# Attention and routed experts on one core: queries kept in a permuted token order, copied out of PSUM in runs of eight

## The chip, the cores and the metric

The kernel runs on one core of one Trainium2 chip. The core has a matrix engine (PE, with its weight loads shown apart as PEld), a vector engine (DVE), an activation engine (ACT), a general engine (POOL, here the issuer of most loads) and a queue engine (SP, which issues the stores). Operands lie in SBUF, 128 partitions wide; matmul results land in PSUM and are copied out by DVE or ACT. The metric is the device time of one execution in microseconds; the figure compared is the median of the runs. Lower is better.

## The reference

Two stages in a row. First attention over 8 batches, 8 heads, 576 tokens and head size 64, with a causal window of 128 tokens and a distance bias per head; then its output, laid out as 4608 tokens by 512, goes through 8 experts. Every expert runs on every token, and the results are added with routing weights that come from eight rounds of row and column normalisation.

```python
scores = scale * np.matmul(q, k.transpose(0, 1, 3, 2))
bias = slopes[:, None, None] * (-np.abs(rel).astype(np.float32))[None, :, :]
mask = (rel >= 0) & (rel < window)
scores = np.where(mask, scores + bias[None], -1000000000.0)
...
attn = attn / (np.sum(attn, axis=-1, keepdims=True) + 1e-09)
return np.matmul(attn, v).astype(np.float32)
...
P = np.exp(logits)
for _ in range(8):
    P /= P.sum(1, keepdims=True) + 1e-09
    P /= P.sum(0, keepdims=True) + 1e-09
    P *= N / E
for e in range(E):
    h = np.maximum(x @ w1[e], 0.0)
    ye = h @ w2[e]
    out += P[:, e:e + 1] * ye
```

The order in which the tokens are held inside is free as long as the rows come out at their places: the experts treat every row alike, and the row sums and column sums of the routing don't depend on the order of the rows.

## The kernel before

**Attention stage.** The work is cut into 40 blocks: 8 batches (b) times 5 key blocks (kb) of 128 keys, the last of 64. Block (b, kb) computes the scores of its keys against the 256 queries from its first key on, so the scores stand with keys on the partitions and queries in the columns (L201). ACT takes the exponential (L209), DVE multiplies by a mask that holds both the window and the bias (L215); the mask `maskT` is a constant of 128 keys by 256 query columns per head, built on the host (L50 to L56). Heads go in two halves of four, and one PSUM tile `psS` serves both halves in turn, so the second half's scores wait for the first half's exponential. One block later the probabilities are multiplied with v (`attend`, L245); the sum of the row comes out as an extra column, DVE takes its reciprocal (L253) and scales (L254) into `xsb`, PE turns `xsb` round (L285) and DVE copies the result into the long-lived `xT` (L294), which holds the tokens in columns for the experts. `gates` (L270) makes the routing logits of 128 tokens as soon as their part of `xT` stands.

**Queries and keys of the next batch.** POOL's queue loads q and k in halves of four heads as tiles `qf` and `kf` (L136), `RT` = 6 tokens per partition, 96 partitions. `turn` (L160, DVE) brings each to a layout in which one token slot of two heads is a block of 128 columns; `tr_unit` (L171) then makes six transposes of 96 x 128 into one PSUM tile `psT`, whose columns run over (slot r, partition i), while the token is 6 i + r. The copies out of PSUM put the tokens into order: ACT copies the keys into `KT` (L180), DVE copies the queries in two halves of 64 partitions into `QZ` (L185, L189), a tile that keeps a zero half for each head of a pair. These copies read `psT` in one run and write every element six elements (12 bytes) from the last one:

```python
out=QZ[0:64, j, 0, :].rearrange("p (i r) -> p r i", r=RT),
in_=psT[0:64],
```

In each batch but the last, blocks kb = 1 to 4 each carry one key unit and one query unit of the next batch, and `turn` follows blocks 0 and 2. Batch 0's own units stand at the start of the program.

**What fills the gaps.** The first expert (e = 0) needs only `xT` and its weights, so its pieces are cut in during the attention stage: a first-layer piece (four matmuls and a Relu on ACT, L92, L99) counts 1, a second-layer piece (eight matmuls of L106 and a DVE copy into the accumulator, L307) counts 2, and each block may spend a credit of `RATE` = 3.45 on them at three places (`fill`). The order of instructions on each engine is the order written in this loop; nothing rearranges it there. The small PSUM tiles (`psT`, `psG`, `psXT`, `psh`, `psy`) share four buffers with the tag `pmm`.

**Expert stage.** After the attention stage come the eight rounds of routing on DVE and POOL, the rest of expert 0, and experts 1 to 7, in groups of 512 tokens: first layer, then per 128 tokens a second layer whose result DVE multiplies by the routing weight and adds to the accumulator (L475). The accumulator of 36 blocks of 128 tokens lies in `acc_lo` (`NHI` = 28 blocks, present from the start) and `acc_hi` (8 blocks, opened after the attention stage). With the last expert each block is stored by one DMA of 256 KB on SP's queue (L484).

Of the kernel before, what the change touches and what calls it, by code (L numbers as in the profile page):

```python
# [14 lines left out]
def kernel(  # L15
# [27 lines left out]
    NPR = H // 2  # L43
    RT = 6
    RATE = 3.45
    RP = S // RT
    scale = float(1.0 / np.sqrt(Dh))

    slopes = 2.0 ** (-8.0 * (np.arange(H, dtype=np.float64) + 1.0) / H)
    _kr = np.arange(P)[:, None, None]  # L50
    _jq = np.arange(2 * P)[None, None, :]
    _rel = _jq - _kr
# [7 lines left out]
    xT = per.tile([P, NDT, Ntok], FP16, name="xT")  # L60
    NHI = 28
    acc_lo = per.tile([P, NHI, HD], FP32, name="acc_lo")
    accs: list = [acc_lo]

    def acc(blk: int):
        return acc_lo[:, blk, :] if blk < NHI else accs[1][:, blk - NHI, :]

    P_sb = per.tile([P, NBLK, E], FP32, name="P_sb")
# [49 lines left out]
    with (  # L118
# [47 lines left out]
        def tr_unit(b: int, nm: str, j: int):  # L166
# [12 lines left out]
            if nm == "k":  # L179
                nc.scalar.copy(  # L180
                    out=KTs[b % 2][:, j, :].rearrange("p (i r) -> p r i", r=RT), in_=psT
                )
            else:
                QZ = QZs[b % 2]
                nc.vector.tensor_copy(  # L185
                    out=QZ[0:64, j, 0, :].rearrange("p (i r) -> p r i", r=RT),
                    in_=psT[0:64],
                )
                nc.vector.tensor_copy(  # L189
                    out=QZ[64:128, j, 1, :].rearrange("p (i r) -> p r i", r=RT),  # L190
                    in_=psT[64:128],
                )
# [106 lines left out]
        def add_group(g: int):  # L299
# [9 lines left out]
            for ft in range(NFT):  # L309
                moe.append((1, lambda ft=ft: l1(ft)))  # L310
            if 4 * g < NHI:
                for ms in range(4):
                    moe.append((2, lambda ms=ms: l2(ms)))
# [96 lines left out]
    with (  # L410
# [28 lines left out]

        for g in range(NG - 2, NG):  # L440
            if g not in hT0:
                hT0[g] = new_hT(0, g, per, "hT", 2)
                for ft in range(NFT):
                    l1_piece(0, g, ft, hT0[g], mps, "psh", 3)
            for ms in range(4):
                psy = l2_mm(0, g, ms, hT0[g], mps, "psy", 4)
                nc.vector.tensor_copy(out=acc(4 * g + ms), in_=psy)
        for e in range(1, E):
# [13 lines left out]
            def emit_l2(g, e=e, hTs=hTs):  # L462
                hT = hTs.pop(g)
                for ms in range(4):
# [18 lines left out]
                    if e == E - 1:  # L483
                        nc.sync.dma_start(  # L484
                            out=out[P * blk : P * blk + P, :], in_=acc(blk)
                        )

# [37 lines left out]
```

## Time and profile before

| what | us |
|---|---|
| median of 3 runs (lowest to highest) | 1250.34 (1248.87 to 1253.21) |
| the profiled execution's own time | 1252.59 |
| its span, first to last instruction | 1250.8 |
| PE busy | 1135.5 (91%) |
| DVE busy | 497.6 (40%) |
| ACT busy | 478.6 (38%) |
| POOL busy | 72.5 (6%) |

The profiled execution lies 2.25 us above the median and 1.8 us above its own span. A matmul's end is modelled, so PE's busy time is not work at PE's peak. In names such as `psT_q_0_1027` the last number is a buffer's, the numbers before it say which piece it is: `psS_1_0_966` is the score tile of kb = 1, first half. Lines L1 to L520 are those of the kernel before. In the view of waits and in the timeline the square brackets hold the idle time of the engine just ahead of an instruction and what ended it.

### The profile page before, as it was taken

How to read it: one execution, taken by the hardware profiler on the slowest of the kernel's cores; microseconds unless marked ns; L12 is line 12 of the kernel's file. 1: busy time of each engine (PE TensorE's matmuls, PEld its weight loads, DVE VectorE, ACT ScalarE, POOL GpSimd, SP SyncE). 2: the span in 40 equal slices, each digit the busy share in tenths (PEclk: the TensorE clock that was granted, in tenths of full speed). 3: DMA queues.
4: the chain of work that ended last, by engine and by line, in shares of the span. 5: the costliest groups of instructions: out<-in, count | busy, mean ns of one | idle time of the engine just before them, and what ended most of it. 6: DMA issues, size and time to landing. Idle time of an engine off the chain costs nothing.

```text
span 1250.8 us, 14241 instructions
## 1 busy us (share of the span) xinstructions
PE 1135.5 (91%) x6032; PEld 530.7 (42%) x6032; DVE 497.6 (40%) x754; ACT 478.6 (38%) x725; POOL 72.5 (6%) x101
## 2 busy tenths in 40 slices
PE   2577678767799999999999999999999999999998
PEld 1334334333344444444444444444444444444443
DVE  7867887778658124122212121212121212121212
ACT  3544445545426430433243324332433243323331
POOL 3212021201000000000000000000000000000000
PEclk9997898888899999999999999999999999999999
DMA  9843354335032020200220022002200220001212
GB/s 137 91 39 40 38 57 38 39 39 63 1 56 47 1 34 1 34 1 1 35 34 1 1 34 34 1 1 35 33 1 1 35 33 1 1 1 56 79 68 101
DMA packets 68912, 41.85 MB, mean 33 GB/s; under 512 B 39536, under 2 KB 60016, under 8 KB 68848
## 3 DMA queue, kind: packets, MB, share of 16 engines
q0 software_dynamic: 63376, 30.95, 20.1%
q1 hardware_dynamic: 5472, 10.00, 2.1%
q8 instruction: 47, 0.77, 0.3%
q14 instruction: 17, 0.14, 0.0%
HBM read 62.44 MB, written 9.44 MB: 57 GB/s over the span
## 4 chain that ended last, share of the span: by engine, by line
PE 81%; DVE 15%; ACT 1%; DMA 1%; issue 1%; POOL 0%; POOLq 0%
DVE QZ_76 L189 3%; DVE QZ_76 L185 3%; DVE QZ_75 L189 2%; DVE QZ_75 L185 2%; DVE xT L294 1%; DVE acc_lo L307 1%; DMA w1t_103<-in_moe_w_dram 1%; DMA kf_0_82<-in_k_dram 0%; POOL vsb_77 L148 0%; PE psy_24_3032 L106 0%; PE psy_20_2623 L106 0%; PE psy_28_3420 L106 0%; PE psy_14_1943 L106 0%; PE psy_2_774 L106 0%; PE psy_19_2362 L106 0%
## 5 line engine op out<-in xcount | busy, mean ns | idle before, releaser
L92 PEld LDWEIGHTS <-w1t_103 128*128 128x128 f16 x288 | 29.1, 109 | 57.9 <-issue 29.1
L92 PEld LDWEIGHTS <-w1t_2981 128*128 128x128 f16 x288 | 28.2, 98 | 34.0
L92 PEld LDWEIGHTS <-w1t_6000 128*128 128x128 f16 x288 | 28.2, 98 | 34.0
L92 PEld LDWEIGHTS <-w1t_6805 128*128 128x128 f16 x288 | 28.2, 98 | 34.0
L92 PEld LDWEIGHTS <-w1t_7610 128*128 128x128 f16 x288 | 28.2, 98 | 34.0
L92 PEld LDWEIGHTS <-w1t_3549 128*128 128x128 f16 x288 | 28.2, 98 | 34.0
L92 PEld LDWEIGHTS <-w1t_4390 128*128 128x128 f16 x288 | 28.2, 98 | 34.0
L92 PEld LDWEIGHTS <-w1t_5195 128*128 128x128 f16 x288 | 28.2, 98 | 34.0
L270 PEld LDWEIGHTS <-xT 128*128 128x128 f16 x144 | 7.0, 100 | 59.0 <-DVE xT L294 56.1
L201 PEld LDWEIGHTS <-KT_73 128*128 128x128 f16 (+1 forms) x80 | 7.8, 113 | 27.4 <-issue 21.0
L148 POOL DMA_DIRECT2D vsb_77<-in_v_dram x20 | 16.9, 867 | 0.4 <-issue 0.4
L148 POOL DMA_DIRECT2D vsb_78<-in_v_dram x20 | 16.9, 868 | 0.0
L99 ACT ACTIVATE hT_0_4394<-psh_0_0_4395 128x512 f16<-128x512 f32 x1 | 0.6, 597 | 41.8 <-PE psh_0_0_4395 L92 41.8
L201 PEld LDWEIGHTS <-KT_74 128*128 128x128 f16 (+1 forms) x80 | 7.0, 105 | 10.7 <-issue 7.2
L467 DVE TENSOR_SCALAR acc_lo<-acc_lo,P_sb 128x512 f32<-128x512 f32 x28 | 11.2, 478 | 0.0
L201 PE MATMUL psS_0_0_158<-QZ_75,KT_73 128*128 128x512 f16 x2 | 1.2, 586 | 6.9 <-DVE QZ_75 L189 6.9
L201 PE MATMUL psS_0_1_202<-QZ_75,KT_73 128*128 128x512 f16 x2 | 1.2, 584 | 6.9 <-DVE QZ_75 L189 6.9
L171 PE MATMUL psT_k_0_124<-ident,kp_0_120 96*128 96x96 f16 x6 | 0.7, 277 | 7.3 <-DVE kp_0_120 L160 7.3
L81 POOL DMA_DIRECT2D w1t_7610<-in_moe_w_dram x1 | 0.8, 752 | 110.1 <-PE psh_8_7_7524 L92 110.1
L81 POOL DMA_DIRECT2D w1t_6805<-in_moe_w_dram x1 | 0.8, 754 | 109.6 <-PE psh_8_7_6719 L92 109.6
L81 POOL DMA_DIRECT2D w1t_6000<-in_moe_w_dram x1 | 0.8, 752 | 109.6 <-PE psh_8_7_5914 L92 109.6
L81 POOL DMA_DIRECT2D w1t_5195<-in_moe_w_dram x1 | 0.8, 752 | 109.6 <-PE psh_8_7_5109 L92 109.6
(2900 smaller groups left out, 2638.7 us busy)
## 6 DMA issues: line engine op xcount, KB each, us to landing
out_dram<-acc_lo SPq DMA_DIRECT2D x28, 256.0 KB, 2.0
vsb_77<-in_v_dram POOLq DMA_DIRECT2D x16, 128.0 KB, 4.7
vsb_78<-in_v_dram POOLq DMA_DIRECT2D x16, 128.0 KB, 5.0
out_dram<-acc_hi SPq DMA_DIRECT2D x8, 256.0 KB, 2.0
w1t_103<-in_moe_w_dram POOLq DMA_DIRECT2D x1, 1024.0 KB, 8.5
w2t_113<-in_moe_w_dram POOLq DMA_DIRECT2D x1, 1024.0 KB, 11.3
w1t_2981<-in_moe_w_dram POOLq DMA_DIRECT2D x1, 1024.0 KB, 9.6
w2t_3362<-in_moe_w_dram POOLq DMA_DIRECT2D x1, 1024.0 KB, 9.1
```

Source lines behind the costliest of these rows:

```text
L81: nc.gpsimd.dma_start(out=w1ts[e], in_=w1v)
L92: nc.tensor.matmul(out=psh, lhsT=w1t[:, dt, P * ft : P * ft + P], rhs=xT[:, dt, GT * g : GT * g + GT], start=(dt == 0), stop=(dt == NDT - 1),)
L99: nc.scalar.activation(out=hT[:, ft, :], in_=psh, func=AF.Relu)
L148: nc.gpsimd.dma_start(out=vsb[0:nk, kb, :, 0:Dh], in_=v[b, :, k0 : k0 + nk, :].rearrange("h s d -> s h d"),)
L171: nc.tensor.matmul(out=psT[:, r, :], lhsT=tt[:, r, 2 * Dh * jj : 2 * Dh * jj + 2 * Dh], rhs=ident[0:RP, 0:RP], is_transpose=True, start=(r ...
L185: nc.vector.tensor_copy(out=QZ[0:64, j, 0, :].rearrange("p (i r) -> p r i", r=RT), in_=psT[0:64],)
L189: nc.vector.tensor_copy(out=QZ[64:128, j, 1, :].rearrange("p (i r) -> p r i", r=RT), in_=psT[64:128],)
L201: nc.tensor.matmul(out=ps[0:nk, jj, :, 0:nq], lhsT=KT[:, 2 * half + jj, k0 : k0 + nk], rhs=QZ[:, 2 * half + jj, :, k0 : k0 + nq],)
L270: nc.tensor.matmul(out=psG, lhsT=xT[:, dt, P * blk : P * blk + P], rhs=wg_sb[:, dt, :], start=(dt == 0), stop=(dt == NDT - 1),)
L294: nc.vector.tensor_copy(out=xT[:, :, t0 : t0 + nk], in_=psXT[:, :, 0:nk])
L307: nc.vector.tensor_copy(out=acc(4 * g + ms), in_=psy)
L467: nc.vector.tensor_scalar(out=acc(blk), in0=acc(blk), scalar1=P_sb[:, blk, 0:1], scalar2=None, op0=ALU.mult,)
```

## The change

`RT` goes from 6 to 8, so q and k are loaded with 8 tokens on each of 72 partitions, and a unit is eight transposes of 72 x 128. `KT` keeps the keys in their own order: ACT now walks `psT` as (i, r), reading two bytes every 144 bytes, and writes one run of 576. `QZ` holds the queries permuted inside each block of 64 tokens: position 8 r + i of a block holds its token 8 i + r. DVE then reads `psT` in its own order and writes runs of 8 elements (16 bytes). The mask's columns take the same permutation; everything behind it (probabilities, `xT`, routing, accumulators) carries its rows in that order, and `store` puts each block of 64 rows back with a DMA of its own, so 72 stores of 128 KB stand in place of 36 of 256 KB. The larger q and k tiles take 5 KB more of each partition; `acc_lo` gives up one block (`NHI` 27), and the second-layer piece of block 27 of expert 0 moves behind the attention stage.

```diff
@@ -41,14 +41,19 @@
     GT = 512
     NG = Ntok // GT
     NPR = H // 2
-    RT = 6
+    RT = 8
+    HB = 64
+    NHB = S // HB
+    HI = HB // RT
     RATE = 3.45
     RP = S // RT
     scale = float(1.0 / np.sqrt(Dh))
 
     slopes = 2.0 ** (-8.0 * (np.arange(H, dtype=np.float64) + 1.0) / H)
+    _pos = np.arange(2 * P)
+    _tok = (_pos // HB) * HB + (_pos % HI) * RT + (_pos % HB) // HI
     _kr = np.arange(P)[:, None, None]
-    _jq = np.arange(2 * P)[None, None, :]
+    _jq = _tok[None, None, :]
     _rel = _jq - _kr
     maskT_np = np.where(
         (_rel >= 0) & (_rel < P), np.exp(-slopes[None, :, None] * _rel), 0.0
@@ -58,12 +63,20 @@
 
     per = ctx.enter_context(tc.tile_pool(name="per", bufs=1))
     xT = per.tile([P, NDT, Ntok], FP16, name="xT")
-    NHI = 28
+    NHI = 27
     acc_lo = per.tile([P, NHI, HD], FP32, name="acc_lo")
     accs: list = [acc_lo]
 
     def acc(blk: int):
         return acc_lo[:, blk, :] if blk < NHI else accs[1][:, blk - NHI, :]
+
+    def store(blk: int):
+        for c in range(P // HB):
+            t0 = P * blk + HB * c
+            nc.sync.dma_start(
+                out=out[t0 : t0 + HB, :].rearrange("(i r) d -> r i d", r=RT),
+                in_=acc(blk)[HB * c : HB * c + HB, :],
+            )
 
     P_sb = per.tile([P, NBLK, E], FP32, name="P_sb")
     ident = per.tile([P, P], FP16, name="ident")
@@ -178,17 +191,18 @@
                 )
             if nm == "k":
                 nc.scalar.copy(
-                    out=KTs[b % 2][:, j, :].rearrange("p (i r) -> p r i", r=RT), in_=psT
+                    out=KTs[b % 2][:, j, :].rearrange("p (i r) -> p i r", r=RT),
+                    in_=psT.rearrange("p r i -> p i r"),
                 )
             else:
                 QZ = QZs[b % 2]
                 nc.vector.tensor_copy(
-                    out=QZ[0:64, j, 0, :].rearrange("p (i r) -> p r i", r=RT),
-                    in_=psT[0:64],
+                    out=QZ[0:64, j, 0, :].rearrange("p (c r i) -> p r c i", r=RT, i=HI),
+                    in_=psT[0:64].rearrange("p r (c i) -> p r c i", i=HI),
                 )
                 nc.vector.tensor_copy(
-                    out=QZ[64:128, j, 1, :].rearrange("p (i r) -> p r i", r=RT),
-                    in_=psT[64:128],
+                    out=QZ[64:128, j, 1, :].rearrange("p (c r i) -> p r c i", r=RT, i=HI),
+                    in_=psT[64:128].rearrange("p r (c i) -> p r c i", i=HI),
                 )
 
         def scores(b: int, kb: int, half: int):
@@ -308,8 +322,8 @@
 
             for ft in range(NFT):
                 moe.append((1, lambda ft=ft: l1(ft)))
-            if 4 * g < NHI:
-                for ms in range(4):
+            for ms in range(4):
+                if 4 * g + ms < NHI:
                     moe.append((2, lambda ms=ms: l2(ms)))
 
         credit = 0.0
@@ -437,12 +451,12 @@
                 op1=ALU.mult,
             )
 
-        for g in range(NG - 2, NG):
+        for g in range(NHI // 4, NG):
             if g not in hT0:
                 hT0[g] = new_hT(0, g, per, "hT", 2)
                 for ft in range(NFT):
                     l1_piece(0, g, ft, hT0[g], mps, "psh", 3)
-            for ms in range(4):
+            for ms in range(max(0, NHI - 4 * g), 4):
                 psy = l2_mm(0, g, ms, hT0[g], mps, "psy", 4)
                 nc.vector.tensor_copy(out=acc(4 * g + ms), in_=psy)
         for e in range(1, E):
@@ -481,9 +495,7 @@
                         op1=ALU.add,
                     )
                     if e == E - 1:
-                        nc.sync.dma_start(
-                            out=out[P * blk : P * blk + P, :], in_=acc(blk)
-                        )
+                        store(blk)
 
             lead = LEAD if e == 1 else 1
             for g in range(min(lead, NG)):
```

On DVE, block (2, 1) of the attention stage. Before (the names ahead of `<-` are written, those behind it read):

```order
L160 COPY qp_0_959<-qf_0_801 96x1536
L215 TENSOR_TENSOR pt_1_0_969<-pt_1_0_969,maskT 128x1024
L215 TENSOR_TENSOR pt_1_1_981<-pt_1_1_981,maskT 128x1024
L253 RECIPROCAL rden_0_0_1004<-psN_2_0_999 128x4
L254 TENSOR_TENSOR xsb_0_998<-psN_2_0_999,rden_0_0_1004 128x256
L253 RECIPROCAL rden_0_1_1012<-psN_2_0_1007 128x4
L254 TENSOR_TENSOR xsb_0_998<-psN_2_0_1007,rden_0_1_1012 128x256
L185 COPY QZ_76<-psT_q_0_1027 64x6x96
L189 COPY QZ_76<-psT_q_0_1027 64x6x96
L294 COPY xT<-psXT_0_1036 128x4x128
```

and now:

```order
L173 COPY qp_0_1007<-qf_0_845 72x2048
L229 TENSOR_TENSOR pt_1_0_1017<-pt_1_0_1017,maskT 128x1024
L229 TENSOR_TENSOR pt_1_1_1029<-pt_1_1_1029,maskT 128x1024
L267 RECIPROCAL rden_0_0_1054<-psN_2_0_1049 128x4
L268 TENSOR_TENSOR xsb_0_1048<-psN_2_0_1049,rden_0_0_1054 128x256
L267 RECIPROCAL rden_0_1_1062<-psN_2_0_1057 128x4
L268 TENSOR_TENSOR xsb_0_1048<-psN_2_0_1057,rden_0_1_1062 128x256
L199 COPY QZ_76<-psT_q_0_1077 64x8x9x8
L203 COPY QZ_76<-psT_q_0_1077 64x8x9x8
L308 COPY xT<-psXT_0_1088 128x4x128
```

No instruction has moved here; the turn has fewer partitions and longer rows, and the query copies have another shape.

On DVE, where the attention stage ends and the routing rounds begin. Before:

```order
L418 TENSOR_REDUCE rs_sb<-P_sb 128x36
L419 RECIPROCAL rs_sb<-rs_sb 128x36
L420 TENSOR_TENSOR P_sb<-P_sb,rs_sb 128x288
L426 TENSOR_REDUCE cs_sb<-P_sb 128x8
L447 COPY acc_hi<-psy_28_3420 128x512
L447 COPY acc_hi<-psy_29_3430 128x512
```

and now:

```order
L432 TENSOR_REDUCE rs_sb<-P_sb 128x36
L433 RECIPROCAL rs_sb<-rs_sb 128x36
L434 TENSOR_TENSOR P_sb<-P_sb,rs_sb 128x288
L440 TENSOR_REDUCE cs_sb<-P_sb 128x8
L461 COPY acc_hi<-psy_27_3538 128x512
L461 COPY acc_hi<-psy_28_3548 128x512
```

The copy of block 27 (and PE's eight matmuls ahead of it) stood inside batch 7 and now opens the pieces behind the attention stage.

On SP, the whole queue from the first store on. Before:

```order
L326 DMA ident<-ident_c 128x128
L328 DMA maskT<-maskT_c 128x2048
L484 DMA out_dram<-acc_lo 128x512 x28
L484 DMA out_dram<-acc_hi 128x512 x8
L520 UNCONDITIONAL_BRANCH
```

and now:

```order
L340 DMA ident<-ident_c 128x128
L342 DMA maskT<-maskT_c 128x2048
L76 DMA out_dram<-acc_lo 8x8x512 x54
L76 DMA out_dram<-acc_hi 8x8x512 x18
L532 UNCONDITIONAL_BRANCH
```

Each store has become two of half the size, and the destination is walked over 8 slots, 8 rows each, of 512 elements.

## The prediction

> **What bounds the kernel now.** I read the page's slices first, then the stretches of time by engine, then the chain of waits inside one attention block.
>
> ```profile
> span 1250.8 us, 14241 instructions
> PE   2577678767799999999999999999999999999998
> DVE  7867887778658124122212121212121212121212
> 118.00:159.00 41.00, 30.10 (x248) 15.67 (x248) 33.13 (x51) 21.46 (x28) 6.91 (x9) 0.88 0.44 44
> 600.00:1251.00 651.00, 646.42 (x2996) 292.88 (x2993) 143.43 (x191) 219.84 (x368) 6.54 (x8) 1.00 0.12 28
> ```
>
> A slice is 31 us. From the thirteenth slice on PE is full: the expert stage is PE's, at 646.42 of 651 us, and nothing in this change touches that work. The first twelve slices are the attention stage, where DVE is the fuller engine (33.13 of 41 us in one batch; the columns behind the length are PE, PEld, DVE, ACT, POOL, granted clock, DMA share). PE's 30.10 us there include matmuls at a lower clock. The chain of waits through block (2, 1) says which DVE work it is:
>
> ```profile
> 118.17 0.55 PE psS_1_0_966 L201 x2
> 118.74 1.03 ACT pt_1_0_969 L209
> 119.81 0.61 PE psS_1_1_978 L201 x2
> 120.44 1.03 ACT pt_1_1_981 L209
> 121.50 0.69 DVE pt_1_1_981 L215
> ...
> 122.86 0.42 DVE xsb_0_998 L254
> 123.29 1.99 DVE QZ_76 L185
> 125.29 2.09 DVE QZ_76 L189
> 127.41 0.43 DVE xT L294
> ```
>
> Scores, exponential, scores, exponential, mask and scaling take 118.17 to 123.28 = 5.1 us; then DVE spends 4.1 us on the two query copies while the next block's logits, and with them PE's in-order queue, wait for the `xT` copy behind them. PE then pays twice:
>
> ```profile
> 144.64 1.86 PE L92 MATMUL psh_2_0_1239<-xT,w1t_103 128*128 128x512 f16 x4 [4.58 <-DVE xT L294]
> 123.98 1.02 PE L92 MATMUL psh_1_7_1042<-xT,w1t_103 128*128 128x512 f16 x4
> ```
>
> After a wait of 4.58 us the same four matmuls take 1.86 us instead of 1.02.
>
> **The copies.** Three rows sum all copies of L185, L189 and L180 in that order (the last holds one table load of 1.28 us besides its 32 copies); two single rows give the comparison.
>
> ```profile
> 0.00:1251.00 1251.00, 66.15 (x32) 0.97 0.22 33
> 0.00:1251.00 1251.00, 66.32 (x32) 0.97 0.22 33
> 0.00:1251.00 1251.00, 67.79 (x33) 0.97 0.22 33
> L294 DVE COPY xT<-psXT_0_1036 x1: 426/426/426, 127.4 to 127.4; 128x512 f16<-128x512 f16 x1
> 125.04 0.60 ACT L99 ACTIVATE hT_1_883<-psh_1_7_1042 128x512 f16<-128x512 f32 x1 [0.63 <-PE psh_1_7_1042 L92]
> ```
>
> A query copy is 2.07 us and a key copy (67.79 - 1.28) / 32 = 2.08 us for 576 elements, 3.6 ns each, on two different engines. Where DVE reads f16 from PSUM in order and writes long runs, 512 elements take 0.43 us. What the slow ones share is the scattered write, 12 bytes apart; so I charge the write. The new query copy reads in order and writes runs of 16 bytes. Bounds: 0.43 x 576/512 = 0.48 us (as good as long runs) and 2.07 us (no gain); nothing excludes even a little more. I take 0.5, since within a run it is the `xT` copy's pattern; 0.8 (no pairing of elements) would alter little, as DVE then still has slack. The 64 copies fall from 132.5 us to 32.
>
> The key copy now writes one run, but reads two bytes every 144 bytes. No row shows such a read of PSUM at length. Bounds: 0.60 x 576/512 = 0.68 us, and 2.08 us if a scattered read costs what a scattered write does. I take 0.9, nearer the lower end, since the one property shown to be slow is gone; the upper end is the first rival. On ACT (21.46 of 41 us) this is off the chain either way, but the copy holds one of the four small PSUM buffers.
>
> **A batch without the stall.** The last batch carries no units, so it shows the loop free of copies. Its blocks, and the first and the last start of kb = 1 in between:
>
> ```profile
> 73.11 0.72 PE L201 MATMUL psS_1_0_551<-QZ_76,KT_74 128*128 128x512 f16 x2
> 329.33 0.61 PE L201 MATMUL psS_1_0_3048<-QZ_76,KT_74 128*128 128x512 f16 x2
> 335.17 0.59 PE L201 MATMUL psS_2_0_3103<-QZ_76,KT_74 128*128 128x512 f16 x2
> 340.98 0.49 PE L201 MATMUL psS_3_0_3169<-QZ_76,KT_74 128*128 128x384 f16 x2
> 346.53 0.30 PE L201 MATMUL psS_4_0_3242<-QZ_76,KT_74 128*64 128x128 f16 x2
> 329.30:346.50 17.20, 15.16 (x118) 7.38 (x116) 10.80 (x26) 8.16 (x12) 0.00 (x0) 1.00 0.00 1
> ```
>
> Six batches take 329.33 - 73.11 = 256.2 us, 42.7 each. Free blocks take 5.84, 5.81 and 5.55 us: the 5.1 us chain plus the turn of `xsb`, with PE busy 15.16 of 17.20 us at full clock. For kb = 0 I take 5.8 (same scores), for kb = 4 5.2 (short exponentials, but the same fill). Sum 28.2 us. What the units add:
>
> ```profile
> 0.00:1251.00 1251.00, 31.77 (x384) 25.12 (x384) 0.97 0.22 33
> L160 DVE COPY kp_0_957<-kf_0_799 x1: 546/546/546, 118.4 to 118.4; 96x1536 f16<-96x1536 f16 x1
> 340.31 0.11 PEld L285 LDWEIGHTS <-xsb_1_3131 128*128 128x128 f16 x2 [1.41 <-DVE xsb_1_3131 L254]
> ```
>
> Transposes (L171): 25.12/384 = 65 ns each by the weight load, so a unit of eight is 0.52 us against 0.39, and a block's two units 1.05 us. About 0.9 of that falls into time in which PE waits for `xsb` in the free blocks (1.41 us in one), since the query unit stands just ahead of that wait; I add 0.2 per block, 0.9 for four, and 0.2 for the key copies' buffer. On DVE the turns grow by 2048/1536 to 0.73 us, 0.7 us per batch, and the query copies are 4.0; with 33.13 - 16.6 + 4.0 + 0.7 = 21.2 us per batch DVE is no bound, and these lie beside the next block's exponentials; if that cover goes, they cost 4.7. So 29.3 us per batch: 6 x (42.7 - 29.3) = **80 us less**. Bounds: 27 (PE's own 15.16 of 17.20 us, all waits gone, plus the transposes) to 34 (rivals).
>
> **The start.** Everything waits for the first eight query copies in series.
>
> ```profile
> 10.27 2.07 DVE L185 COPY QZ_75<-psT_q_0_132 64x576 f16<-64x576 f16 x1 [0.76 <-PE psT_q_0_132 L171]
> 13.15 7.73 DMA w1t_103<-in_moe_w_dram
> 20.94 0.56 DVE kp_1_164 L160
> 31.10 0.58 PE L201 MATMUL psS_0_1_202<-QZ_75,KT_73 128*128 128x512 f16 x1 [3.50 <-DVE QZ_75 L189]
> 60.68 1.06 PE L201 MATMUL psS_0_0_474<-QZ_76,KT_74 128*128 128x512 f16 x2
> ```
>
> Eight copies at 1.57 us less would give 12.6 us by 31.1, but the chain has the second turn at 20.94 beside a load that ends at 20.9; if that load holds it, only four copies count, 6.3. I take 7. From 31.1 to 60.68 batch 0 runs slow matmuls (1.06 us for a pair that takes 0.59 later) and the next batch's loads still come in, so of eight more copies I count 5 us, and 4 between 60.68 and 73.11, where one more pair stands ahead of an `xT` copy. In all **16 us less**, bounds 8 and 24.
>
> **What is added.** Block 27's eight matmuls (1.89 us, the first row) leave batch 7 and come behind it, and the block they leave shrinks by somewhat less, as its chain of 5.1 us stays; +1. The stores:
>
> ```profile
> 335.60 1.89 PE L106 MATMUL psy_27_3109<-w2t_113,hT_6_2812 128*128 128x512 f16 x8
> L484 SPq DMA_DIRECT2D out_dram<-acc_hi x8: 332/332/333, 1235.2 to 1247.2; - x8
> out_dram<-acc_hi SPq DMA_DIRECT2D x8, 256.0 KB, 2.0
> q1 hardware_dynamic: 5472, 10.00, 2.1%
> ```
>
> Only the last pair lies bare; the others run under PE's work, and nothing on SP waits but stores. The second half of the pair is issued 0.33 us after the first, and lands between that and 2.0 us later than one store does now; I take +1. [...]
>
> **Sum.** 1252.6 (the profiled execution's own time) - 80 - 16 + 2 = 1158.6, and brought to the median of the runs, 2.25 us lower, 1156.
>
> **The rivals.**
> *The key copy stays slow.* The strided read of PSUM costs 2.1 us as the strided write did. For: nothing shows such a read to be fast, and the buffer already binds now and then:
>
> ```profile
> 123.56 0.38 PE L285 MATMUL psXT_0_1036<-ident,xsb_0_998 128*128 128x128 f16 x4 [0.56 <-ACT KT_74 L180]
> ```
>
> With shorter blocks that wait would come in each of 28 units, and the next exponential would start late: 0.56 + 0.2 each, some 21 us: 1177 (1168 to 1198, the upper end with a copy twice as slow). Against: the slow copies both read in order, so what was slow was the write. [...] Chance 0.20.
> *PE becomes the bound early.* If the denser stage is granted 0.88 of the clock, as in 118 to 159 now, a batch takes 29.3/0.88 = 33.3 us: 1180. Against: 1.00 in the free blocks, and the low clock stands beside the waits. Chance 0.07.
> *Slower: the copies cost what they did.* If a copy's time is set by leaving a transposed PSUM tile and not by its writes, DVE's queue between `xsb` and `xT` stays as it is, and gains 28 turns x 0.18 = 5 us, PE 64 x 0.13 = 8 us of transposes, of which some half is bare, and the 2 us above: 1250 + 11 = 1261. It decides from a query copy of about 1.95 us on. Against: the `xT` copy leaves a transposed tile in 0.43 us. Chance 0.03.
> That the gain is used up by loads at the start and by waits not seen, and nothing is left, has 0.02.
>
> **How the numbers follow.** My forecast has 0.68, with 1140 to 1168 as its own range. To hold 8 in 10 the range must take in most of the first two rivals: 1134 to 1190. Differences under 0.3% can't be told from none here. Faster by more than that: 0.68 + 0.20 + 0.07 = 0.95; the same 0.02; slower 0.03.
>
> **What would show it.** Right: query copies near 0.5 us, DVE near 21 us per batch, kb = 1 to kb = 1 in 29 us, the chain through the stage running PE, ACT, DVE mask and scaling, and no more 4 us waits for `xT`. Wrong: key copies of 2 us with PE waiting for `KT`; blocks over 6.5 us with DVE below half; a batch at a granted clock under 0.95; a first score of (1, 1) later than 65 us; or an expert stage that is longer than before by more than 3 us.

## The result, and the profile after

The changed kernel takes 1154.96 us (median; 1153.14 to 1155.11) against 1251.26 us (1248.87 to 1253.21) for the kernel before, run beside it on the same chip: a ratio of 0.9228, 95% interval 0.9208 to 0.9248. The forecast was 1156 us.

The page of the changed kernel, its span and two of its rows of slices (now 29 us each):

```profile
span 1153.1 us, 14537 instructions
PE   3899899989999999999999999999999999999997
DVE  5667777757523412222222222221222122222222
```

PE was at 2 to 8 tenths in its first eleven slices; from the second to the ninth it now stands at 8 or 9, and the last attention block begins in the ninth slice (243.33 us). The starts of kb = 1 in batches 1, 4 and 7, from the order of time on PE:

```profile
52.31 0.61 PE L215 MATMUL psS_1_0_583<-QZ_76,KT_74 128*128 128x512 f16 x2
169.76 0.61 PE L215 MATMUL psS_1_0_2325<-QZ_76,KT_74 128*128 128x512 f16 x2
226.52 0.60 PE L215 MATMUL psS_1_0_3176<-QZ_76,KT_74 128*128 128x512 f16 x2
```

Two stretches of time by engine (length, then PE, PEld, DVE, ACT, POOL, granted clock, DMA share, GB/s): the six batches from start to start, of before and of after.

```profile
73.10:329.30 256.20, 189.54 (x1482) 97.61 (x1480) 199.05 (x307) 131.07 (x165) 40.14 (x52) 0.87 0.42 43
```

```profile
52.31:226.52 174.21, 160.09 (x1578) 88.79 (x1577) 126.19 (x307) 94.97 (x165) 41.22 (x52) 0.99 0.61 63
```

Where the 97.7 us between the two profiled executions (1252.59 and 1154.86) went:

| stretch | before | after | difference | predicted |
|---|---|---|---|---|
| start to (1, 1) | 73.11 | 52.31 | -20.8 | -16 |
| six batches, (1, 1) to (7, 1) | 256.2 | 174.2 | -82.0 | -80 |
| (7, 1) to the end of the span | 921.5 | 926.6 | +5.1 | +2 |

A batch takes 174.2 / 6 = 29.0 us instead of 42.7. Over the six, PE is busy 160.09 of 174.21 us at a granted clock of 0.99, and DVE, at 126.19, is no longer the fuller engine. The chain from block (4, 1) on, after:

```profile
169.83 0.54 PE psS_1_0_2325 L215 x2
170.37 1.73 PE psy_16_2331 L119 x8
172.10 0.45 PE psS_1_1_2341 L215 x2
172.57 1.03 ACT pt_1_1_2344 L223
173.62 0.69 DVE pt_1_1_2344 L229
...
175.47 0.29 PE psXT_0_2395 L299 x2
175.76 0.43 PE psS_2_0_2401 L215 x2
...
181.83 0.36 DVE QZ_75 L199
182.20 0.46 DVE QZ_75 L203
182.69 0.42 DVE xT L308
```

One block takes 175.76 - 169.83 = 5.9 us and PE's fill stands in the chain. Where the query copies come into the chain at all, they cost it 0.36 and 0.46 us, not 1.99 and 2.09. The longest wait of PE for `xT` between 55 and 230 us, in the table of waits (us in total, times, longest), is 1.4 us; before, one of 4.58 was quoted.

```profile
PE psh_2_0_1299 L105 <- DVE xT L308: 1.4, 1, 1.4
```

The copies themselves, in the lists of instructions (lowest, middle, highest ns):

```profile
L199 DVE COPY QZ_75<-psT_q_0_134 x1: 450/450/450, 12.1 to 12.1; 64x576 f16<-64x576 f16 x1
L193 ACT COPY KT_73<-psT_k_2_176 x1: 638/638/638, 17.8 to 17.8; 128x576 f16<-128x576 f16 x1
```

### The profile page after: what moved, and what is told of

Same layout as the page of the kernel before. It is cut to its first block, busy times and chain, and to the rows that moved or that the text cites. A ratio compares the mean times of both kernels' runs of the same rounds, so it can differ in the third digit from the quotient of the medians.

```text
span 1153.1 us, 14537 instructions
## 1 busy us (share of the span) xinstructions
PE 1105.6 (96%) x6160; PEld 521.9 (45%) x6160; DVE 400.4 (35%) x754; ACT 430.5 (37%) x725; POOL 74.5 (6%) x101
## 4 chain that ended last, share of the span: by engine, by line
PE 88%; DVE 6%; ACT 3%; DMA 1%; issue 1%; POOL 1%; POOLq 0%; DVEq 0%
DMA qf_0_107<-in_q_dram 1%; DMA kf_0_82<-in_k_dram 1%; DVE acc_lo L321 1%; POOL vsb_77 L161 0%; DVE xT L308 0%; PE psy_27_3538 L119 0%; PE psy_28_3548 L119 0%; DVE QZ_75 L203 0%; PE psy_24_3160 L119 0%; PE psy_3_857 L119 0%; PE psy_35_9404 L119 0%; PE psy_11_1682 L119 0%; PE psy_0_722 L119 0%; PE psy_34_9392 L119 0%; PE psy_32_9368 L119 0%
## 5 line engine op out<-in xcount | busy, mean ns | idle before, releaser
L105 PEld LDWEIGHTS <-w1t_4518 128*128 128x128 f16 x288 | 28.2, 98 | 34.0
L105 PEld LDWEIGHTS <-w1t_3677 128*128 128x128 f16 x288 | 28.2, 98 | 34.0
L105 PEld LDWEIGHTS <-w1t_5323 128*128 128x128 f16 x288 | 28.2, 98 | 34.0
L105 PEld LDWEIGHTS <-w1t_6933 128*128 128x128 f16 x288 | 28.2, 98 | 34.0
L105 PEld LDWEIGHTS <-w1t_7738 128*128 128x128 f16 x288 | 28.2, 98 | 34.0
L105 PEld LDWEIGHTS <-w1t_3109 128*128 128x128 f16 x288 | 28.2, 98 | 34.0
L105 PEld LDWEIGHTS <-w1t_6128 128*128 128x128 f16 x288 | 28.2, 98 | 34.0
L105 PEld LDWEIGHTS <-w1t_103 128*128 128x128 f16 x288 | 26.1, 99 | 34.4 <-DVE xT L308 4.7
L215 PEld LDWEIGHTS <-KT_73 128*128 128x128 f16 (+1 forms) x80 | 7.7, 110 | 17.2 <-issue 13.8
L481 DVE TENSOR_SCALAR acc_lo<-acc_lo,P_sb 128x512 f32<-128x512 f32 x27 | 10.8, 485 | 0.0
```

The costliest lines, as they stand in the source:

```text
L105: nc.tensor.matmul(out=psh, lhsT=w1t[:, dt, P * ft : P * ft + P], rhs=xT[:, dt, GT * g : GT * g + GT], start=(dt == 0), stop=(dt == NDT - 1),)
L215: nc.tensor.matmul(out=ps[0:nk, jj, :, 0:nq], lhsT=KT[:, 2 * half + jj, k0 : k0 + nk], rhs=QZ[:, 2 * half + jj, :, k0 : k0 + nq],)
L481: nc.vector.tensor_scalar(out=acc(blk), in0=acc(blk), scalar1=P_sb[:, blk, 0:1], scalar2=None, op0=ALU.mult,)
```

## The experiments

The change joins several edits: six slots become eight, the key copy is turned round, the query copies write runs of eight, the rows are put back at the store, block 27 is moved. My theory was that the scattered write was dear and the scattered read is not; the rival was that the read of PSUM costs too. Below, a kernel "on after" or "on before" is that kernel with only the edit shown. To cut the time at a place that all kernels have, I use the first score of kb = 4 in batches 0 and 7; what lies behind the second one is called the rest.

**The query copies scattered again (q_old, on after).** Natural order, eight slots, plain stores (cut: the second half of the query copy alike, the store as in store_plain below):

```diff
-    _tok = (_pos // HB) * HB + (_pos % HI) * RT + (_pos % HB) // HI
+    _tok = _pos
...
-    out=QZ[0:64, j, 0, :].rearrange("p (c r i) -> p r c i", r=RT, i=HI),
-    in_=psT[0:64].rearrange("p r (c i) -> p r c i", i=HI),
+    out=QZ[0:64, j, 0, :].rearrange("p (i r) -> p r i", r=RT),
+    in_=psT[0:64],
```

> The changed kernel with the query copies alone as before: natural query order, PSUM read in order, scattered writes; mask in natural order and one plain store per block; the fast key copy, 8 tokens per partition and NHI 27 stay. Theory 1 (the whole gain is the query copies'): a batch stays at 42 to 43 us with DVE at 33 us of it, total 1250 to 1262 us (turns and transposes that grew lie on the bound engine). Rival (the key copy carries a good part of the gain): 1200 to 1240 us.

Measured: 1310.49 us, ratio 1.0476 (1.0454 to 1.0497). The direction is the theory's, the size is not. One group of instructions (lowest, middle, highest ns), and one batch (columns as above):

```profile
L194 DVE COPY QZ<-psT_q x32: 2680/2700/2721, 12.0 to 376.5; 64x576 f16<-64x576 f16 x32
```

```profile
164.40:213.00 48.60, 34.30 (x258) 16.99 (x257) 38.32 (x51) 15.90 (x26) 7.10 (x9) 0.79 0.35 34
```

A copy that writes 16 bytes apart takes 2.70 us, not the 2.07 of 12 bytes apart, and a batch 50.5 us on the mean of six (48.6 in the one shown). So the six-slot kernel before wasn't the worst case, and going to eight slots without the new copies loses 59 us. The longer copies are 64 x 0.63 = 40 us of that; what the longer turns and the lower clock (0.79 in the batch shown) take of the rest isn't separated. The two prices, 2.07 and 2.70 us, give a guess: a charge for each 16-byte stretch that the copy enters. At 16 bytes apart each element enters a new one, at 12 bytes three in four: with 0.17 us fixed, (2.70 - 0.17) x 0.75 + 0.17 = 2.07. That guess is tested further on.

**The key copy scattered again (k_old, on after).**

```diff
-    out=KTs[b % 2][:, j, :].rearrange("p (i r) -> p i r", r=RT),
-    in_=psT.rearrange("p r i -> p i r"),
+    out=KTs[b % 2][:, j, :].rearrange("p (i r) -> p r i", r=RT),
+    in_=psT,
```

> The changed kernel with the key copy on ACT written as before: PSUM read in order, one element every 16 bytes into KT. Both theories expect 2.0 to 2.1 us per key copy and query copies unchanged at 0.45 us. Theory 1 (the price in the prediction): the slow key copy holds its small PSUM buffer and delays the next exponential, 0.5 to 0.8 us in each of 28 units, 15 to 21 us, so 1170 to 1176 us. Theory 2: ACT has room enough (its busy time in a batch stays near 22 of 29 us) and the copy is off the chain: within 5 us of the changed kernel, 1155 to 1160 us.

Measured: 1165.65 us, ratio 0.9316 (0.9294 to 0.9338): 10.7 us more than after, between the two expectations, which both had this copy at 2.0 to 2.1 us. With eight slots it too is dearer than it was; behind its group stands its row in the table of PE's waits from 55 to 230 us:

```profile
L193 ACT COPY KT<-psT_k x32: 2702/2725/3040, 8.6 to 230.1; 128x576 f16<-128x576 f16 x32
```

```profile
PE psXT L299 <- ACT KT L193: 3.1, 5, 1.2
```

2.72 us instead of 0.64 gives 10.7 / 28 = 0.38 us per unit, where the rival had 0.76. The wait that the rival named exists, but comes 5 times, 3.1 us in all; with two smaller rows of the same table, ten waits of PE end with this copy, 5.0 us. Where the rest of the 10.7 us lies isn't shown. This isn't the old copy's price of 2.08; the next three kernels have that one.

**On before, the copies turned round one by one (k_only, q_only, dense_both).** No permutation, six slots, plain stores, `NHI` = 28. The key edit and the query edit (second half alike); k_only has the first, q_only the second, dense_both both:

```diff
-    out=KTs[b % 2][:, j, :].rearrange("p (i r) -> p r i", r=RT), in_=psT
+    out=KTs[b % 2][:, j, :].rearrange("p (i r) -> p i r", r=RT),
+    in_=psT.rearrange("p r i -> p i r"),
...
-    out=QZ[0:64, j, 0, :].rearrange("p (i r) -> p r i", r=RT),
-    in_=psT[0:64],
+    out=QZ[0:64, j, 0, :].rearrange("p (i r) -> p i r", r=RT),
+    in_=psT[0:64].rearrange("p r i -> p i r"),
```

> The kernel before with the key copy alone turned round (PSUM read every 192 bytes, KT written in one run), query copies scattered as before. Theory (DVE's query copies alone set the stage): key copies 0.64 us, batches still 41 to 42 us, total 1244 to 1252 us. Rival (key and query copies share the delay): 1220 us or less.

> The kernel before with the query copies alone turned round (natural order, written in one run), key copies scattered as before at 2.08 us. Theory: nearly all the gain, less what a slow key copy costs once DVE is out of the way (the key copy at 2.70 us cost 10.7 us, so at 2.08 us some 7): 1160 to 1166 us. Rival (the two copies must both be fast before PE gains): 1190 us or more.

> The kernel before (6 tokens per partition, natural order everywhere, plain stores, NHI 28) with both copies turned round: PSUM read scattered (every 192 bytes), SBUF written in one run. Theory 1 (only scattered writes are slow, on DVE as on ACT): query copy 0.7 to 0.8 us (no pairing of elements), key copy 0.64 us, DVE about 23 us per batch and so no bound: batches of 28.5 to 29.5 us, total 1148 to 1156 us, no slower than the changed kernel. Rival (the permutation is needed because DVE reads PSUM slowly when scattered): query copies at 1.5 us or more, total 1190 to 1260 us.

| kernel | median us | ratio (95% interval) | query copies us | key copy us | first score of (0, 4) / (7, 4) us | rest us |
|---|---|---|---|---|---|---|
| before | 1251.26 | 1 | 2.07 | 2.08 | 53.80 / 346.53 | 904.3 |
| k_only | 1251.88 | 1.0004 (0.9993 to 1.0016) | 2.07 | 0.64 | 53.88 / 344.77 | 904.5 |
| q_only | 1157.78 | 0.9247 (0.9232 to 0.9263) | 0.75 | 2.09 | 41.22 / 251.81 | 902.9 |
| dense_both | 1156.82 | 0.9244 (0.9220 to 0.9267) | 0.75 | 0.64 | 40.58 / 247.07 | 904.6 |
| after | 1154.96 | 0.9228 (0.9208 to 0.9248) | 0.45 | 0.64 | 41.98 / 243.33 | 909.8 |

Three things follow. First, the gain is that of DVE's query copies: turning the key copy gives nothing while DVE's stall stands. Once the stall is gone, a key copy of 2.09 us costs little: q_only lies below its expectation of 1160 us, and 1.0 us above dense_both by medians whose intervals overlap (in the profiled executions (7, 4) starts 4.7 us later). Second, the permuted order isn't needed: dense_both, which reads PSUM two bytes in every 192 and writes in order, ties with the change. Its batches are longer (206.5 / 7 = 29.5 us against 28.8) and its rest is shorter by 5.2 us. Third, in these kernels the scattered read has a price on DVE only: 0.75 us for 576 elements instead of 0.45, while ACT's 0.64 us lies below the 0.68 reckoned by length from a read in order. What these kernels don't separate is the clock: eight query copies at 1.62 us less are 13.0 us of the 13.7 that a batch lost, and the granted clock rose from 0.87 to 0.99 in the same stretch, but no run changes one without the other. The key copies of k_only in one batch, and the second halves of dense_both's query copies over the whole run (busy us, mean ns, idle before and its releaser):

```profile
L180 ACT COPY KT<-psT_k 128x576 f16<-128x576 f16 x4 | 2.6, 640 | 0.8 <-PE psT_k L171 0.8
```

```profile
L190 DVE COPY QZ<-psT_q 64x576 f16<-64x576 f16 x32 | 24.3, 760 | 0.4
```

**Half of the query copies moved to ACT (dense_split, on dense_both).**

```diff
-    nc.vector.tensor_copy(
+    nc.scalar.copy(
         out=QZ[64:128, j, 1, :].rearrange("p (i r) -> p i r", r=RT),
```

> Both copies turned round in natural order, and the second half of each query copy moved from DVE to ACT. If DVE's 0.75 us copies are what keeps that kernel's batch at 29.5 us instead of 28.8, DVE now has less to do than in the changed kernel, a batch takes 28.8 us and the total is 1149 to 1153 us. If ACT's longer queue takes it back (1.3 us of copies ahead of the next exponential), 1156 to 1162 us.

Measured: 1154.58 us, ratio 0.9218 (0.9203 to 0.9233): 2.2 us below dense_both's median, with intervals that overlap, and level with after. The median lies between the two expectations. Batches take 208.9 / 7 = 29.8 us, no less than with both on DVE, so DVE's 0.75 us copies were not what kept them at 29.5. Once DVE has slack, where the copies lie hardly matters.

**The price of a copy by itself (micro).** A kernel that does nothing of the computation: it fills one PSUM tile and copies 576 f16 elements per partition out of it, on DVE (names with v) and ACT (names with s). The write step is the distance in elements; runs stand 64 bytes apart.

```diff
+for s, nm in ((1, "a"), (2, "b"), (3, "c"), (4, "d"), (6, "e"), (8, "f"), (16, "g")):
+    o = sb.tile([P, N, s], FP16, name=f"{en}wstep{nm}", tag="o", bufs=2)
+    cp(out=o[:, :, 0], in_=psT)
+for n, nm in ((2, "b"), (4, "d"), (8, "f"), (16, "g")):
+    o = sb.tile([P, N // n, 32], FP16, name=f"{en}wrun{nm}", tag="o", bufs=2)
+    cp(out=o[:, :, 0:n], in_=psT.rearrange("p (c n) -> p c n", n=n))
+for r, nm in ((2, "b"), (6, "e"), (8, "f")):
+    o = sb.tile([P, N // r, r], FP16, name=f"{en}rstep{nm}", tag="o", bufs=2)
+    cp(out=o, in_=psT.rearrange("p (r i) -> p i r", r=r))
```

> Not the computation: only copies of one PSUM tile (128 x 576, f16) to SBUF, each form twice on DVE (names begin with v) and twice on ACT (s); the output is zeros. Forms: written every 1, 2, 3, 4, 6, 8, 16 elements (wstep a to g); in runs of 2, 4, 8, 16 elements 64 bytes apart (wrun b, d, f, g); read every 288, 96, 72 elements (rstep b, e, f), written in one run; and the transposed write every 8 elements (swstep f). Line theory, fitted to 2.07 us at 12 bytes and 2.70 us at 16: a fixed 0.17 us plus the larger of the element rate and 4.4 ns for every 16-byte stretch of SBUF entered: steps 1, 2, 3, 4, 6, 8, 16 give on DVE 0.46, 0.80, 1.12, 1.44, 2.07, 2.70, 2.70 us, on ACT 0.65, 0.80, 1.12, 1.44, 2.07, 2.70, 2.70; runs of 2, 4, 8, 16 give 1.44, 0.80, 0.49, 0.47 on DVE and 1.44, 0.80, 0.65, 0.65 on ACT. Rival (every element that doesn't follow the last one costs the same): steps 2, 3, 4 near 2 us too, and the step of 16 above that of 8. Scattered reads: 0.75 us on DVE, 0.64 on ACT, whatever the step.

The first dense copy in the order of time, then groups of instructions (means of two rounds): single elements 8, 12, 16 and 32 bytes apart on DVE, 16 apart on ACT; then runs of 2 and 4; then reads scattered over eight slots with a dense write.

```profile
8.59 0.46 DVE L91 COPY vwstepa<-pst 128x576 f16<-128x576 f16 x1 [2.39 <-PE pst L72]
...
L91 DVE COPY vwstepd<-pst 128x576 f16<-128x576 f16 x2 | 2.8, 1420 | 0.0
L91 DVE COPY vwstepe<-pst 128x576 f16<-128x576 f16 x2 | 4.2, 2100 | 0.0
L91 DVE COPY vwstepf<-pst 128x576 f16<-128x576 f16 x2 | 5.7, 2826 | 0.0
L91 DVE COPY vwstepg<-pst 128x576 f16<-128x576 f16 x2 | 5.5, 2770 | 0.0
L91 ACT COPY swstepf<-pst 128x576 f16<-128x576 f16 x2 | 6.0, 3010 | 0.0
...
L94 DVE COPY vwrunb<-pst 128x576 f16<-128x576 f16 x2 | 1.7, 828 | 0.0
L94 DVE COPY vwrund<-pst 128x576 f16<-128x576 f16 x2 | 0.9, 430 | 0.0
...
L97 DVE COPY vrstepf<-pst 128x576 f16<-128x576 f16 x2 | 1.5, 742 | 0.0
L97 ACT COPY srstepf<-pst 128x576 f16<-128x576 f16 x2 | 1.6, 800 | 0.0
```

For single elements the guess holds: 0.17 us and 4.4 ns for each 16-byte stretch entered gives 1.44, 2.07, 2.70 and 2.70 us for 288, 432, 576 and 576 stretches; measured are 1.42, 2.10, 2.83 and 2.77. For runs it falls: two adjacent elements, 288 stretches, take 0.83 us and not 1.44; four, 144 stretches, take 0.43 and not 0.80. So what is charged is not the stretch as such; with two adjacent elements the charge is about half (0.83 - 0.17 = 0.66 us for 288 stretches, 2.3 ns each), and with four nothing of it is left (0.43 us). Several writes to one stretch are not the reason by themselves: at 8 bytes apart each of the 288 stretches gets two single elements, as in the runs of two, and the copy still takes 1.42 us. What differs is that the two stand side by side. By these rows a run of four (0.43 us) would have served the query copies as well as the change's eight (0.44); no kernel tried it. Reads scattered at any step tried (2, 6, 8) take 0.74 us on DVE. On ACT they take 0.77 to 0.80 us by the means of the two rounds, where runs of four and more, read in order, took 0.73 to 0.76 and the copy in order 0.87.

**The rows not put back (store_plain, on after).** The kernel leaves out the return of the rows to their places.

```diff
-    for c in range(P // HB):
-        t0 = P * blk + HB * c
-        nc.sync.dma_start(
-            out=out[t0 : t0 + HB, :].rearrange("(i r) d -> r i d", r=RT),
-            in_=acc(blk)[HB * c : HB * c + HB, :],
-        )
+    nc.sync.dma_start(out=out[P * blk : P * blk + P, :], in_=acc(blk))
```

> The changed kernel with one store of 256 KB per block in the order in which the rows are held; putting the rows back is left out. Theory 1: of the 5 us that the time behind (7, 1) has grown, the pair of stores costs its share at the end only: from the last issue to the end 3.6 us again instead of 5.0, total 1 to 2 us below the changed kernel. Rival: the 72 half stores also slow the stream in the last expert: 3 us or more below.

Measured: 1153.28 us, ratio 0.9217 (0.9201 to 0.9233), 1.7 us below after by the medians, with intervals that overlap. In the profiled executions the rest is 906.3 against 909.8 us, 3.5 less. The last sum on DVE in the order of time, then the transfers from 1140 to 1154 us in 40 slices (tenths of the 16 engines), of store_plain (span 1152.1 us):

```profile
1147.77 0.75 DVE L484 SCALAR_TENSOR_TENSOR acc_hi<-psy,P_sb,acc_hi 128x512 f32<-128x512 f32 x1 [0.98 <-PE psy L114]
```

```profile
DMA  0089100891009900098001980019800000000000
```

The same of after (its span stands above):

```profile
1146.64 0.75 DVE L489 SCALAR_TENSOR_TENSOR acc_hi<-psy_35_9404,P_sb,acc_hi 128x512 f32<-128x512 f32 x1 [0.98 <-PE psy_35_9404 L119]
```

```profile
DMA  2444534445345454454444545345444100000000
```

Plain stores come in bursts at 8 to 9 tenths of the engines and are done before the next block. The halves run at 3 to 5 tenths without a pause, and the last pair starts right behind the one before it. From the start of that sum to the end of the span it is 1152.1 - 1147.8 = 4.3 us with plain stores (as before: 1250.8 - 1246.5 = 4.3) and 1153.1 - 1146.6 = 6.5 with halves. That is 2.1 of the 3.5 us. What is left lies at the other end: where the attention stage ends, the granted clock is about a half for 6.9 us in after's profiled execution and for 3.4 us in store_plain's.

```profile
249.80:256.70 6.90, 6.25 (x20) 2.31 (x21) 2.94 (x6) 0.18 (x1) 0.39 (x1) 0.51 0.59 97
```

```profile
253.30:256.70 3.40, 3.35 (x9) 1.22 (x9) 1.96 (x4) 0.00 (x1) 0.40 (x1) 0.53 0.84 138
```

At half the clock, 3.5 us more are some 1.7 us of matmul time, an estimate. This stretch doesn't go with the stores: it is 6.8 us in q_old, which has plain stores, 3.4 in before and none in q_only and dense_split. So the halves cost about 2 us, at the end.

**The second halves from another queue (store_two, on after).**

```diff
-            nc.sync.dma_start(
+            eng = nc.sync if c == 0 else nc.scalar
+            eng.dma_start(
```

> The changed kernel with the second half store of each block issued from ACT's queue instead of SP's. If the pair's extra time at the end (6.5 us from the last DVE instruction to the end, 4.3 with one plain store) is the second issue on SP (0.6 us): about 0.6 us less, 1154 to 1155 us, and 5.9 us at the end. If both halves run on the same transfer engines in series, the issue gains nothing more than that; if halves on two queues run side by side, 4.5 to 5 us at the end. A loss is possible too: 0.6 us of issue per block on ACT, ahead of the Relus of the last expert.

Measured: 1154.34 us, ratio 0.9230 (0.9214 to 0.9245), no difference from after that can be told. Its span is 1152.1 us, its last sum starts at 1145.4, and its transfers are these:

```profile
DMA  4546445554555444544544554442000000000000
```

The tail is still 6.7 us, and the transfers, from two queues now, still stand at 4 to 6 tenths. So it isn't SP's time of issue that holds them (0.60 us per half by the next row, of after, against 0.33 for a whole block), but the transfers themselves; why they stand at about half isn't shown.

```profile
L76 SPq DMA_DIRECT2D out_dram<-acc_hi x18: 603/604/604, 1126.7 to 1148.1; - x18
```

**More and less fill (split_rate40, split_rate29, on dense_split).** Since PE is the fuller engine of the stage now, I changed how much of expert 0 is cut in: `RATE = 3.45` becomes 4.0 and 2.9.

> The kernel with both copies turned round and half of each query copy on ACT, with RATE 4.0 instead of 3.45, so more pieces of expert 0 are cut into the attention stage. Theory 1 (the stage now has idle PE time that more pieces fill: PE is busy 134.8 of 152.1 us over five batches): 3 to 5 us less, 1150 to 1152 us. Theory 2 (every piece lengthens its block by what it takes, since PE sets the block): within 2 us of 1154.6.

> The same kernel with RATE 2.9: fewer pieces in the stage, about 22 of some 138 credits of 0.86 us moved behind it. Theory 1 (idle PE time that is lost): 8 to 15 us more, 1163 to 1170 us. Theory 2 (PE sets the block): the blocks get shorter by what leaves them, within 3 us of 1154.6.

Measured: 1188.51 us at 4.0 (ratio 0.9501, 0.9478 to 0.9523) and 1162.89 at 2.9 (0.9297, 0.9280 to 0.9315), against 1154.58 at 3.45. At 2.9 the attention stage reaches (7, 4) 6.3 us earlier and the rest grows by 15.4: 8.3 us more by the medians, as theory 1 has it (8 to 15). So of the 15.4 us of work, 9.1 had found free time in the stage, and PE's work sets the blocks only in part. At 4.0 the loss of 34 us was expected by neither theory. Stretches of dense_split, then of split_rate40, the last two inside its first:

```profile
60.00:250.00 190.00, 169.12 (x1537) 92.22 (x1534) 123.79 (x296) 111.66 (x192) 34.58 (x45) 0.99 0.51 54
```

```profile
60.00:250.00 190.00, 163.30 (x1366) 86.36 (x1365) 109.86 (x259) 100.21 (x172) 34.58 (x45) 0.89 0.51 54
250.00:300.00 50.00, 39.93 (x285) 19.32 (x284) 24.01 (x60) 15.76 (x29) 1.28 (x2) 0.80 0.14 22
126.00:133.00 7.00, 4.36 (x49) 2.47 (x48) 4.64 (x10) 3.28 (x5) 1.97 (x3) 1.00 1.63 132
133.00:144.00 11.00, 8.63 (x54) 3.98 (x54) 5.76 (x14) 4.35 (x8) 1.34 (x2) 0.53 0.41 55
```

In the same 190 us PE gets through 1366 instructions instead of 1537, at a granted clock of 0.89 instead of 0.99, and from 250 to 300 us at 0.80, where dense_split's mean over the whole run is 0.999. By estimate, if PE always had work, 0.10 of 190 us and 0.20 of 50 us are 29 of the 34 us lost. Each batch frees 16 x 9 / 8 = 18 units of fill (nine groups of eight first-layer pieces at 1 and four second-layer pieces at 2, over eight batches), while a rate of 4.0 asks for 5 x 4.0 = 20; at 3.45 it is 17.25. Counted through the loop, that leaves one or two blocks of each batch, from batch 1 on, with at most one unit. The last two rows show such a place: PE is busy 4.36 of 7.00 us, and in the 11 us behind it the clock is 0.53. That the clock fell, and that idle time stands ahead of it, is shown; that the one causes the other isn't.

## Why the prediction was right, step by step

**The copies.** Query copies 0.5 us: measured 0.45. The turn 0.73: 0.68. The key copy was taken at 0.9, nearer the lower bound; it is 0.64, a little below that bound of 0.68, so the read costs ACT nothing that shows. The reason given, that the scattered write was slow, is what micro shows, on both engines: 2.10 us on DVE and 2.25 on ACT for elements 12 bytes apart. For single elements a charge per stretch of 16 bytes fits; two elements in a stretch (0.83 us in runs of two, 1.42 us at 8 bytes apart) still take longer than the 0.43 of runs of four. The 0.8 that stood beside the 0.5 is near 576/512 of the 0.68 us in which DVE of before copies 512 f32 elements out of PSUM (L307), 0.77 by estimate; a pairing of elements as its ground is not shown.

**A batch.** 29.3 us forecast, 29.0 measured. The size is right; the path is so only in part. The forecast had scores, exponentials, mask and scaling set the block, with fill beside them; in the chain above, PE's fill stands among them, and PE is busy 0.92 of the six batches where the free blocks had 0.88. The transposes, taken at 65 ns by the weight load, are shorter than that with 72 partitions:

```profile
0.00:1154.00 1154.00, 30.03 (x512) 24.95 (x512) 0.99 0.24 36
```

512 of them take 24.95 us of weight load, 49 ns each, the same sum as 384 before (25.12 us), so a unit of eight is 0.39 us where I had reckoned 0.52. The clock, a rival's ground, is 0.99 over the six batches, and DVE's forecast of 21.2 us per batch is 126.19 / 6 = 21.0. Two slips in the working moved nothing much: 0.2 us for each of four blocks is 0.8, not 0.9, and the bound of 27 us doesn't follow from its parts (15.16 / 17.20 of 28.2 us is 24.9, and eight units at 0.52 us add 4.2).

**The start.** Forecast -16 with bounds -8 and -24, measured -20.8. The step that was too small is the first one: I let the second turn, beside a load, hold the chain and counted 7 of 12.6 us ahead of the last score of block (0, 0). That score now starts at 20.32 us instead of 31.10, 10.8 earlier:

```profile
20.32 0.59 PE L215 MATMUL psS_0_1_218<-QZ_75,KT_73 128*128 128x512 f16 x1 [0.28 <-DVE QZ_75 L203]
```

The load held nothing. In both kernels the second turn follows on DVE right behind the first mask product, which waits for the exponential (two rows of before, then two of after):

```profile
20.33 0.69 DVE L215 TENSOR_TENSOR pt_0_0_161<-pt_0_0_161,maskT 128x1024 f16<-128x1024 f16 x1 [1.73 <-ACT pt_0_0_161 L209]
20.94 0.55 DVE L160 COPY kp_1_164<-kf_1_86 96x1536 f16<-96x1536 f16 x1
```

```profile
15.73 0.69 DVE L229 TENSOR_TENSOR pt_0_0_169<-pt_0_0_169,maskT 128x1024 f16<-128x1024 f16 x1 [1.73 <-ACT pt_0_0_169 L223]
16.34 0.68 DVE L173 COPY kp_1_172<-kf_1_86 72x2048 f16<-72x2048 f16 x1
```

So all eight copies count: from the first copy to that score it is 31.10 - 10.27 = 20.8 us before and 20.32 - 12.10 = 8.2 after, 12.6 less. Of that 1.8 us are lost because the first copy starts later; the first turn, which waits for its load, starts at 8.24 us instead of 6.70. The net 10.8 is 3.8 more than taken; the later 10.0 us are the 9 forecast.

**What is added.** Forecast +2, measured +5.1: this term was mis-sized. Of it -0.4 lies between (7, 1) and (7, 4), 17.2 and 16.8 us, and +5.5 behind. By the profiled executions three things make up the 5.5, where I had 1 for the stores and 1 for the moved block: about 2.1 for the stores at the end (6.5 against 4.3), some 1.7 for the half clock behind the attention stage (6.9 us of it against 3.4 before), and what is left, 1.7, for the moved block, whose eight matmuls take 1.89 at full clock. Each is good to 1 or 2 us only, since the rests of the five kernels that leave the block where it was run from 902.9 to 904.6. The stores' step reckoned with the last pair alone, while the slices above show transfers without a pause, so that the last pair starts behind the one before. At the 150 GB/s or so that the profile gives for these slices (117 to 187 from 1141 to 1150 us) a pair of 256 KB takes about 1.75 us, by estimate. The moved block's matmuls take nearly twice what they did in the stage (3.57 us against 1.89):

```profile
250.95 3.57 PE L119 MATMUL psy_27_3538<-w2t_113,hT_6_2932 128*128 128x512 f16 x8 [0.26 <-ACT P_sb L291]
```

I had priced them at the rate they had between full blocks. They lie in the stretch of half clock shown above. Before, block 28 was the first behind the stage and took 3.20 us, so the slow clock there isn't the move's doing; why it lasts twice as long in some executions isn't shown. It was a term that the sum didn't have.

**The rivals.** "The key copy stays slow" isn't the case (0.64 us), and its price was far too high: a copy of 2.09 us costs about 1 us by the medians (q_only against dense_both, no difference that can be told), not 21. Even at 2.72 us it costs 10.7. The wrong step was to let the wait fall on each of 28 units: in k_old ten waits of PE end with the copy. "PE becomes the bound early" is half right: PE is now the fuller engine, but at 0.99 of the clock. "Slower" has no ground, since the query copies take 0.45 us; a slower kernel does exist one edit away, but by another cause: eight slots with the old query copies, writing 16 bytes apart, give 1310 us. The first rival's ground, that a scattered read of PSUM costs what the scattered write did, about 2.1 us, the traces don't show: it is 0.64 us on ACT, and one element per 1.3 ns on DVE (0.74 us for 576).

Errors of both signs met in the sum. Against the profiled execution it came out at 1158.6 for 1154.86, 3.7 too high: the start held 4.8 us more gain than taken and the batches 2.0, what is added 3.1 more loss. Then I took off 2.25 us, as the profiled execution of before stood above its median; that of after stands at it (1154.86 and 1154.96). So the nearness of 1156 to 1154.96 is partly luck, and better than its terms.

## What to carry to other kernels

When a copy out of PSUM has to change the order of elements, scatter the read and write in order (here 0.75 us on DVE instead of 2.07, and 0.64 on ACT instead of 2.08): then no permuted order, and no store that undoes one, is needed (dense_both ties with the change). Where the order may be permuted, runs of four 2-byte elements were as fast as longer ones (0.43 us on DVE, against 0.44 for runs of 8 and 16). Look for which engine's copies the stall waits: the same edit was worth 94 us on DVE's copies and nothing on ACT's. Before splitting a store, look at how full it keeps the DMA engines (here the halves stand at 3 to 5 tenths, the whole blocks at 8 to 9), and reckon with the blocks just ahead of the last one too. And look at the granted clock of a stretch before pricing matmuls that move into it (at 0.51 eight of them took 3.57 us instead of 1.89).

## What the runs showed of the hardware

- In micro, single 2-byte elements cost some 4.4 ns for each 16-byte stretch of SBUF that the copy enters, on DVE and, a little more, on ACT (2.83 and 3.01 us for 576 elements 16 bytes apart, 2.10 and 2.25 at 12); 16 bytes apart is dearer than 12 (2.70 against 2.07 us in the kernels), and 32 bytes apart costs no more than 16 (2.77 and 2.99 us).
- Two adjacent elements halve that there (0.83 us in 288 runs on DVE), two single ones in the same stretch don't (1.42 us); in runs of four nothing is left of it (0.43 us, against 0.46 us of the first dense copy in the same kernel).
- A read of PSUM scattered over 2, 6 or 8 slots takes 0.74 us on DVE, where copies in order take 0.43 to 0.46; on ACT it takes 0.64 us in the kernels, and by itself 0.77 to 0.80, against 0.73 to 0.76 for copies read in order and written in runs of four and more.
- The 128 KB stores, written 8x8x512, stand at 3 to 5 tenths of the DMA engines' time without a pause from one queue (after) and at 4 to 6 from two (store_two); the plain ones of 256 KB stand at 8 to 9 tenths in bursts. An issue takes 0.60 us of SP for a half (after) and 0.33 for a whole block (store_plain).
- Asking for a little more fill than there is (4.0 instead of 3.45 per block) cost 34 us, with a granted clock of 0.89 from 60 to 250 us, where dense_split has 0.99, and of 0.80 from 250 to 300 us.
- Behind the attention stage the granted clock is about a half for 6.9 us in after (0.51), 3.4 in store_plain (0.53) and not at all in q_only and dense_split; eight matmuls there take 3.57 us in after instead of 1.89.
